# High parts of converted units five steps behind their sums, low parts of weights one step behind, unit stores on GpSimd

## The chip, the cores and the metric

One Trainium2 chip, one of its cores. The core has TensorE (PE; PEld is its weight load), VectorE (DVE), ScalarE (ACT), GpSimd (POOL) and SyncE (SP), which run their own instruction streams in order and wait for one another by semaphores; DMA queues are issued from SP and from POOL. The metric is the device time of one execution in microseconds, as a median of runs. Lower is better.

## The reference

Three stages on 3072 tokens (4 batches of 768) of width 512, all in float32:

```
attention: 8 heads of 64, chunks of 32 queries against 16 + 32 + 8 keys and 8 memory keys, softmax
experts:   tokens with x @ w_skip > 0 go to e = argmax(x @ w_gate);
           x += gate * (relu(x @ w1[e]) @ w2[e])      w1: 512 x 1024, w2: 1024 x 512, 8 experts
dense:     h = max(x @ m1, x @ m2, x @ m3);  out = h @ mo         512 x 768 and 768 x 512
```

The weights of the dense stage (m1, m2, m3, mo) arrive as 64 bit floats.

## The kernel before

To multiply float32 at TensorE's faster rate, each operand is split into a high part (a rounded copy, made by ScalarE) and a low part (operand minus high part, made by VectorE), and a product is three matmuls: high by high, high by low, low by high.

**Experts.** Function `experts` runs eight experts, e = 0 to 7, each with the 256 tokens (two tiles of 128) that were gathered for it. The first product has eight pieces f of 12 matmuls (512 to 1024, into `hp`), the second eight pieces f times two token halves h of 3 matmuls (into `yp`). Between them the tokens of expert e + 1 are transposed (`trans`, tiles `tp`, `xh`, `xl`). The relu leaves `hp` as `hh` (ScalarE) and `hl` (VectorE). `finish(i, y)` multiplies `yp` of the expert before by the gate and adds it to the token rows `xr` on VectorE (L410), and scatters them to `xn` in DRAM from GpSimd (L412); it stands at pieces f = 2 and 3 of the next expert's first product (`FIN`). There is one `yp` per half, so the second product of expert e cannot start before `finish` of expert e - 1 has read it.

**Weights.** Class `Weights` cuts w1 and w2 of an expert into eight units of 128 x 1024. `load` fetches a unit into one of 7 staging tiles (`stga`, `stgb`) from SP, `split` makes the high part (L136, ScalarE) into one of 8 pairs, and `low` the low part (L147, VectorE), after which the staging tile is free again. At each even f the loop calls `K.split(2, upto=i + AHEAD)`, with AHEAD = 5 units, and `K.load()`.

**Conversions.** Beside the experts, class `Convert` turns the 64 bit weights of the dense stage into float32, in units of 128 x 512. The generator `steps` does one unit: an absolute value on ScalarE (`cg<-craw`, L201), six VectorE instructions up to the sum (L203 to L215, tiles `cg` and `cs`), then `lag` steps later the high part (L225, ScalarE) and the low part (L226, VectorE). `feeder` starts a unit every CP = 6.9 steps and advances all units that are under way by one step per call; an expert makes 16 calls (`next(conv)`), 4 in the first product and 12 in the second. Units 0 to 8 stay in SBUF (`unit`); units 9 to 15 go to DRAM (`away`): their high part is made in the one tile `cx`, their low part in `cg` itself, of which there are two, and both are stored (L231). The last expert, e = 7, does its second product half by half, transposes four tiles of tokens for the dense stage meanwhile (`x0`, loaded at L444, transposed at L503), and adds its own result to them by a matmul.

**Dense.** `dense` starts with blocks of 512 tokens j = 0 and 1. `first(j, f)` makes the three products of a piece f of 128 hidden columns, w = 0, 1, 2, each 12 matmuls (L577, into `gp`), and keeps the maximum (`hm`). After each product `step` advances the conversions and the sums that are left. The four token tiles of block 1 are transposed and split by `trans(t)` (`dtp`, `dxh` L566, `dxl` L567) inside `first(0, 1)` and `first(0, 2)`, at the places that `turns` names. `first(1, 0)` needs all four.

The order of the instructions on each engine is the order in which this code calls them.

Of the kernel before, what the change touches and what calls it, by code (L numbers as in the profile page):

```python
# [9 lines left out]
F32 = mybir.dt.float32  # L10
# [19 lines left out]
NEG = -1.0e30  # L30
BIG = float(1 << 20)
TOK0 = 8192.0
AHEAD, C0, CP, LP, LAG = 5, 10, 6.9, 3.2, 2
FIN = (2, 3)
W0, W1, W2, W3, W4 = 7, 0, 4, 4, (0, 3)
CAP = 256
# [118 lines left out]
class Convert:  # L155
# [39 lines left out]
    def steps(self, pool, u, last, lag, fine):  # L195

        nc, V, t = self.nc, self.nc.vector, self.raw.pop(u)
        L, Hw = t[:, :, 0], t[:, :, 1]
        g = pool.tile([128, 512], F32, name="cg", bufs=self.depth)
        gu = g.bitcast(U32)  # L200
        nc.scalar.activation(out=g, in_=Hw.bitcast(F32), func=AF.Abs)  # L201
        yield
        V.tensor_scalar(g, g, 2.0 ** -15, 2.0 ** 16, ALU.max, ALU.mult)  # L203
        V.tensor_scalar(gu, gu, 4, 1, ALU.logical_shift_left, ALU.logical_shift_right)
        if fine:
            yield
        V.scalar_tensor_tensor(out=gu, in0=Hw, scalar=0x80000000, in1=gu, op0=ALU.bitwise_and, op1=ALU.bitwise_or)
        yield
        s = pool.tile([128, 512], U32, name="cs", bufs=self.depth - 1)
        r = s.bitcast(F32)  # L210
        V.tensor_scalar(s, gu, 0xFF800000, None, ALU.bitwise_and)
        V.scalar_tensor_tensor(out=r, in0=L, scalar=2.0 ** -52, in1=r, op0=ALU.mult, op1=ALU.mult)
        if fine:
            yield
        V.tensor_tensor(out=g, in0=g, in1=r, op=ALU.add)  # L215
        if u + self.depth < last:
            self.load(pool, u + self.depth)
        for _ in range(lag):
            yield
        if u < len(self.unit):  # L220
            d = self.unit[u]
            hi, lo = (d[:, c].rearrange("p k f -> p (k f)") if len(d.shape) == 4 else d[:, c] for c in range(2))
        else:
            hi, lo = pool.tile([128, 512], F32R, name="cx", bufs=1), g.bitcast(F32R)
        nc.scalar.copy(hi, g)  # L225
        V.tensor_tensor(out=lo, in0=g, in1=hi.bitcast(F32), op=ALU.subtract)  # L226
        if u < len(self.unit):
            self.done.add(u)
        else:
            for c, x in enumerate((hi, g)):  # L230
                nc.sync.dma_start(out=self.away[u][:, c * 512:(c + 1) * 512], in_=x.bitcast(F32))  # L231

    def feeder(self, pool, units, start, period, lag, fine=True):

# [118 lines left out]
def order(late):  # L353

    if late:
        return [(c, k) for k in range(4) for c in (0, 1)] + [(2, k) for k in range(4)]
    return [(c, k) for k in range(4) for c in range(3)]
# [16 lines left out]
def experts(ac, tc, nc, env):  # L374
    K, C, tab, xn, ident, gidx, sidx = map(env.__getitem__, ("K", "C", "tab", "xn", "ident", "gidx", "sidx"))
# [28 lines left out]
    def passes(ah, al, bh, bl):  # L404
        return ((ah, bh), (ah, bl), (al, bh))
# [3 lines left out]
    def finish(i, y):  # L409
        nc.vector.scalar_tensor_tensor(out=xr[i], in0=y, scalar=tab[:, 1, col(i)], in1=xr[i],  # L410
                                       op0=ALU.mult, op1=ALU.add)
        nc.gpsimd.indirect_dma_start(  # L412
            out=xviews[i], out_offset=bass.IndirectOffsetOnAxis(ap=sidx[:, col(i)], axis=0),
            in_=xr[i], in_offset=None, bounds_check=NT - 1, oob_is_err=False)
# [5 lines left out]
    for e in range(NE):  # L420
        hh = pool.tile([128, 8, 256], F32R, name="hh")
        hl = pool.tile([128, 8, 256], F32R, name="hl")
        for f in range(8):
            if f % 2 == 0:
                i = 8 * e + f // 2
                K.split(2, upto=i + AHEAD)
                K.load()
                wh, wl = (w.rearrange("p (k f) -> p k f", k=4) for w in K.hl[i])
                hp = ps.tile([128, 2, 256], F32, name="hp", bufs=4)
            sl = slice((f % 2) * 128, (f % 2) * 128 + 128)  # L430
            for n, (c, k) in enumerate(order(e == 0 and f == 0)):
                a, b = ((wh, xh[e]), (wl, xh[e]), (wh, xl[e]))[c]
                nc.tensor.matmul(hp[:, f % 2], lhsT=a[:, k, sl], rhs=b[:, k, :], start=(n == 0), stop=(n == 11))  # L433
            if f % 2:
                F = slice(f - 1, f + 1)
                nc.scalar.activation(out=hh[:, F], in_=hp, func=AF.Relu)
                nc.vector.scalar_tensor_tensor(out=hl[:, F], in0=hp, scalar=0.0, in1=hh[:, F].bitcast(F32),  # L437
                                               op0=ALU.max, op1=ALU.subtract)
            if f in FIN and done:
                finish(*done.pop(0))  # L440
            if e == NE - 1 and f == 4:
                x0 = [xrp.tile([128, DM], F32, name="xr") for _ in range(4)]
                for t in range(4):
                    nc.sync.dma_start(out=x0[t], in_=xn[t * 128:(t + 1) * 128, :])  # L444
            if f % 2:
                next(conv, None)
                K.free(i)
        if e + 1 < NE:
            trans(e + 1)
        yp = [ps.tile([128, 512], F32, name=f"yp{h}", bufs=1) for h in range(2)]  # L450

        def gemm2(f, h):
            wh, wl = (w.rearrange("p (f d) -> p f d", f=2) for w in K.hl[8 * e + 4 + f // 2])
            sl = slice(h * 128, h * 128 + 128)
            for n, (a, b) in enumerate(passes(hh[:, f, sl], hl[:, f, sl], wh[:, f % 2, :], wl[:, f % 2, :])):
                nc.tensor.matmul(yp[h], lhsT=a, rhs=b, start=(f == 0 and n == 0), stop=(f == 7 and n == 2))  # L456

        if e == NE - 1:
            break
        for f in range(8):  # L460
            if f % 2 == 0:
                i = 8 * e + 4 + f // 2
                K.split(2, upto=i + AHEAD)
                K.load()
                if f == 2 and 1 <= e and e + 2 < NE:
                    gather(nc, xrp, xr, xn, gidx, e + 2)
            for h in range(2):
                gemm2(f, h)
            next(conv, None)
            if f % 2:  # L470
                next(conv, None)
                K.free(i)
        done = [(2 * e + h, yp[h]) for h in range(2)]
# [56 lines left out]
def dense(ac, tc, nc, env):  # L530
# [6 lines left out]
    C, xn, out, ident, dram = map(env.__getitem__, ("C", "xn", "out", "ident", "dram"))  # L537
# [16 lines left out]
    def load_pair(j, t):  # L554
        load(j, t, [b * 512 + t * 128 for b in (j, j + 1)])
# [120 lines left out]
    steps = [(0, f) for f in range(3)] + [(1, f) for f in range(3)]  # L676
    steps += [(j, f) for f in range(3, 6) for j in range(2)]
    for j, f in steps:
        turns = (2 * f - 2, 2 * f - 1) if j == 0 and f in (1, 2) else ()
        first(j, f, late=(j, f) == (0, 0), step=step, turns=turns)  # L680
        if (j, f) in ((1, 0), (1, 1), (1, 2)):
            load_pair(2, f)
# [797 lines left out]
```

## Time and profile before

| | us |
|---|---|
| median of 3 runs | 766.55 |
| lowest and highest | 765.63 and 767.0 |
| the profiled execution | 766.06 |
| its span, first to last instruction | 764.3 |
| PE busy / DVE busy / ACT busy / POOL busy in it | 707.9 / 546.2 / 292.6 / 133.5 |
| mean granted TensorE clock | 0.983 |

Attention takes the first 167 us, the experts run from there to about 376, the dense stage from there to the end. A row of the timeline shows one instruction: its start, its duration, engine, line, operation, tiles, and in brackets how long its engine had been idle before it and what ended that. Instructions of an engine overlap a little, so what one costs its engine is the distance from its start to the next start, where nothing waits. The profiled execution is 0.49 us below the median.

### The profile page before, as it was taken

The numbers are of one execution on the slowest core, as the hardware profiler recorded it, in microseconds if no ns is written. First come the engines' busy times: TensorE is split into PE (matmuls) and PEld (weight loads), VectorE is DVE, ScalarE is ACT, GpSimd is POOL, SyncE is SP. The second block draws the span as 40 slices with busy tenths as digits, with TensorE's granted clock in tenths as the row PEclk, the third lists the DMA queues.
The fourth block names the chain that finished last, engine by engine and source line by source line (L and its number), as shares of the span: only waits on it lengthen the run. The fifth ranks groups of instructions, "written<-read, shape, count | busy, mean of one in ns | idle before, by whom it ended". The sixth has DMA issues, their size and how long they took to land.

```text
span 764.3 us, 13711 instructions
## 1 busy us (share of the span) xinstructions
PE 707.9 (93%) x5209; PEld 598.6 (78%) x5209; DVE 546.2 (71%) x1027; ACT 292.6 (38%) x498; POOL 133.5 (17%) x273
## 2 busy tenths in 40 slices
PE   6677888969999999989998999999999999999998
PEld 5656677759888899868787888788888888888876
DVE  6455767875799999899689895665666774666641
ACT  5455756534545665344433223450000262000031
POOL 7335546312022121212101111000000000000000
PEclk9999999979999999999999999999999999999999
DMA  8799999838978788873384775212453411333211
GB/s 222 152 243 213 222 229 213 199 124 280 314 253 275 268 267 278 296 252 117 122 330 185 276 257 192 70 56 96 166 194 137 155 67 56 138 138 138 69 42 69
DMA packets 118547, 140.76 MB, mean 184 GB/s; under 512 B 34574, under 2 KB 84750, under 8 KB 118192
## 3 DMA queue, kind: packets, MB, share of 16 engines
q1 hardware_dynamic: 112608, 121.37, 51.7%
q0 software_dynamic: 5872, 18.49, 6.7%
q8 instruction: 42, 0.69, 0.4%
q14 instruction: 25, 0.20, 0.1%
HBM read 103.30 MB, written 32.24 MB: 177 GB/s over the span
## 4 chain that ended last, share of the span: by engine, by line
PE 46%; issue 13%; DMA 11%; DVE 5%; POOL 2%; ACT 1%; SPq 0%; POOLq 0%; DVEq 0%; ACTq 0%
PE gp L761 23%; PE dtp L607 13%; PE gp L577 10%; DMA xr<-xn,gidx 4%; DMA xn<-xr,sidx 3%; DMA craw<-in_moe_w_out_dram 1%; DMA stgb<-in_moe_w_dram 1%; POOL xn L412 1%; DVE wloa L147 1%; PE gp L560 1%; DVE wlob L147 1%; DMA craw<-in_moe_w_dram 1%; DVE hl L437 1%; DMA xs<-xn 1%; DVE xr L410 0%
## 5 line engine op out<-in xcount | busy, mean ns | idle before, releaser
L765 DVE TENSOR_TENSOR tmp<-tmp,gp 128x512 f32<-128x512 f32 x102 | 70.0, 686 | 49.9 <-PE gp L761 49.7
L607 PE MATMUL dtp<-unit,hp 128*128 128x512 f32 x432 | 101.4, 392 | 1.5 <-DVE hp L592 1.5
L607 PEld LDWEIGHTS dtp<-unit,hp 128*128 128x128 f32 x432 | 80.1, 188 | 19.1 <-DVE hp L592 2.3
L433 PE MATMUL hp<-xh,whia 128*128 128x256 f32 x256 | 72.2, 282 | 0.0
L433 PE MATMUL hp<-xh,wloa 128*128 128x256 f32 x256 | 72.0, 281 | 0.0
L433 PE MATMUL hp<-xl,whia 128*128 128x256 f32 x256 | 71.4, 281 | 0.0
L781 ACT COPY tmp<-gp 128x512 f32<-128x512 f32 x18 | 10.6, 588 | 146.4 <-PE gp L761 128.5
L456 PE MATMUL yp<-whib,hh 128*128 128x512 f32 x128 | 52.1, 407 | 5.8 <-DVE xr L410 5.8
L456 PE MATMUL yp<-wlob,hh 128*128 128x512 f32 x128 | 50.7, 396 | 0.0
L456 PE MATMUL yp<-whib,hl 128*128 128x512 f32 x128 | 50.5, 395 | 0.0
L433 PEld LDWEIGHTS hp<-xh,whia 128*128 128x128 f32 x256 | 48.8, 191 | 0.3
L433 PEld LDWEIGHTS hp<-xh,wloa 128*128 128x128 f32 x256 | 48.7, 190 | 0.3
L433 PEld LDWEIGHTS hp<-xl,whia 128*128 128x128 f32 x256 | 48.3, 190 | 0.0
L761 PE MATMUL gp<-unit,set 128*128 128x512 f32 x180 | 46.9, 395 | 0.0
L577 PE MATMUL gp<-x0h,unit 128*128 128x512 f32 x144 | 43.5, 393 | 1.3 <-ACT x0h L522 1.3
L761 PE MATMUL gp<-x0h,unit 128*128 128x512 f32 x144 | 44.5, 390 | 0.0
L577 PE MATMUL gp<-dxh,unit 128*128 128x512 f32 x144 | 44.4, 389 | 0.0
L412 POOL DMA_INDIRECT xn<-xr,sidx x16 | 18.9, 1181 | 132.0 <-DVE xr L410 131.1
L761 PEld LDWEIGHTS gp<-unit,set 128*128 128x128 f32 x180 | 33.7, 187 | 8.2
L1043 PE MATMUL xp<-vs,pb 128*64 128x65 f32 x736 | 28.0, 230 | 10.2 <-DMA vs<-vs 2.7
L592 DVE TENSOR_TENSOR hp<-hm,hp 128x768 fp32r<-128x768 f32 (+2 forms) x26 | 22.9, 895 | 19.8 <-ACT hp L591 19.6
L761 PE MATMUL gp<-unit,unit 128*128 128x512 f32 x144 | 36.5, 389 | 0.0
(272 smaller groups left out, 1619.7 us busy)
## 6 DMA issues: line engine op xcount, KB each, us to landing
stga<-in_moe_w_dram SPq DMA_DIRECT2D x38, 512.0 KB
stgb<-in_moe_w_dram SPq DMA_DIRECT2D x26, 512.0 KB
set<-sum SPq DMA_DIRECT2D x20, 512.0 KB
craw<-in_moe_w_dram SPq DMA_DIRECT2D x18, 512.0 KB
unit<-sum SPq DMA_DIRECT2D x16, 512.0 KB
k<-in_k_dram SPq DMA_DIRECT2D x12, 512.0 KB
q<-in_q_dram SPq DMA_DIRECT2D x12, 512.0 KB
out_dram<-ob SPq DMA_DIRECT2D x24, 256.0 KB
```

What stands on the lines that cost most here:

```text
L147: self.nc.vector.tensor_tensor(out=lo, in0=t, in1=hi.bitcast(F32), op=ALU.subtract)
L412: nc.gpsimd.indirect_dma_start(out=xviews[i], out_offset=bass.IndirectOffsetOnAxis(ap=sidx[:, col(i)], axis=0), in_=xr[i], in_offset=None, ...
L433: nc.tensor.matmul(hp[:, f % 2], lhsT=a[:, k, sl], rhs=b[:, k, :], start=(n == 0), stop=(n == 11))
L437: nc.vector.scalar_tensor_tensor(out=hl[:, F], in0=hp, scalar=0.0, in1=hh[:, F].bitcast(F32), op0=ALU.max, op1=ALU.subtract)
L456: nc.tensor.matmul(yp[h], lhsT=a, rhs=b, start=(f == 0 and n == 0), stop=(f == 7 and n == 2))
L577: nc.tensor.matmul(gp[w], lhsT=l_[:, k, :], rhs=r_[:, k, :], start=(n == 0), stop=(n == 11))
L592: V.tensor_tensor(out=p[:, 1, F], in0=m, in1=p[:, 0, F].bitcast(F32), op=ALU.subtract)
L607: nc.tensor.matmul(op, lhsT=l_, rhs=r_, start=(f == 0 and c == 0), stop=(f == 5 and c == 2))
L761: nc.tensor.matmul(acc, lhsT=l_[:, i, :], rhs=r_[:, i, :], start=(n == 0), stop=(n == 5))
L765: V.tensor_tensor(out=o, in0=x, in1=y, op=ALU.add)
L781: nc.scalar.copy(u, m1)
L1043: nc.tensor.matmul(xps[t][hd // 4][cp * 64:cp * 64 + 64, (hd % 4) * (D + 1):(hd % 4 + 1) * (D + 1)], lhsT=pb[:, hd // 2, cp, hd % 2, :], r ...
```

## The change

The number of steps between the sum of a unit and its high part rises from 2 to 5 in the experts (`LAG`). The stores of the units that go to DRAM are issued from GpSimd, not from SyncE. At each even f, the low parts of the weight units whose high parts were made at the even f before are made first, then new high parts (`split` with `low=False`), then the loads. In the dense stage, tile 2 of block 1 is transposed after w = 2 of `first(0, 1)` and tile 3 after w = 0 of `first(0, 2)`; before, they stood after w = 0 and w = 1 of `first(0, 2)`.

```diff
-AHEAD, C0, CP, LP, LAG = 5, 10, 6.9, 3.2, 2
+AHEAD, C0, CP, LP, LAG = 5, 10, 6.9, 3.2, 5
...
             for c, x in enumerate((hi, g)):
-                nc.sync.dma_start(out=self.away[u][:, c * 512:(c + 1) * 512], in_=x.bitcast(F32))
+                nc.gpsimd.dma_start(out=self.away[u][:, c * 512:(c + 1) * 512], in_=x.bitcast(F32))
...
                 i = 8 * e + f // 2
-                K.split(2, upto=i + AHEAD)
+                K.low()
+                K.split(2, upto=i + AHEAD, low=False)
                 K.load()
...
                 i = 8 * e + 4 + f // 2
-                K.split(2, upto=i + AHEAD)
+                K.low()
+                K.split(2, upto=i + AHEAD, low=False)
                 K.load()
...
-        turns = (2 * f - 2, 2 * f - 1) if j == 0 and f in (1, 2) else ()
+        turns = {1: (0, 1, 2), 2: (3,)}.get(f, ()) if j == 0 else ()
```

On VectorE, around `finish` of expert 0 (tiles `xr`), early in the first product of expert 1, this stands in a row before (`wlob` are low parts of weights, `unit<-cg` the low part of conversion unit 0):

```order
L147 TENSOR_TENSOR wlob_3189<-stgb_3183,whib_3188 128x1024
L437 SCALAR_TENSOR_TENSOR hl<-hp,hh 128x512
L226 TENSOR_TENSOR unit_3166<-cg,unit_3166 128x512
L147 TENSOR_TENSOR wlob_3191<-stgb_3184,whib_3190 128x1024
L410 SCALAR_TENSOR_TENSOR xr<-yp_3388,tab,xr 128x512
L437 SCALAR_TENSOR_TENSOR hl<-hp,hh 128x512
L410 SCALAR_TENSOR_TENSOR xr<-yp_3389,tab,xr 128x512
```

and this in the changed kernel (its lines below L426 are one or two higher):

```order
L147 TENSOR_TENSOR wlob_3187<-stga_80,whib_3186 128x1024
L438 SCALAR_TENSOR_TENSOR hl<-hp,hh 128x512
L147 TENSOR_TENSOR wlob_3189<-stgb_3183,whib_3188 128x1024
L410 SCALAR_TENSOR_TENSOR xr<-yp_3386,tab,xr 128x512
L438 SCALAR_TENSOR_TENSOR hl<-hp,hh 128x512
L410 SCALAR_TENSOR_TENSOR xr<-yp_3387,tab,xr 128x512
```

The low part of unit 0 has moved behind the two `xr`, and each low part of weights stands where its forerunner stood.

On GpSimd, in experts 5 to 7, seven pairs of stores now stand among the gathers (L368) and the scatters (L412); this is the stretch from the scatters of expert 4 to those of expert 6, of the changed kernel:

```order
L412 DMA xn<-xr,sidx 3072x512 [waits DVE_49]
L231 DMA away_3159<-cx 128x512 [waits Activation_49]
L231 DMA away_3159<-cg 128x512 [waits DVE_49]
L368 DMA xr<-xn,gidx 128x512 [waits DMASW1_49,DMASW0_49,PE_49]
L368 DMA xr<-xn,gidx 128x512 [waits PE_49]
L231 DMA away_3160<-cx 128x512 [waits Activation_49]
L231 DMA away_3160<-cg 128x512 [waits DVE_49]
L231 DMA away_3161<-cx 128x512 [waits Activation_49]
L231 DMA away_3161<-cg 128x512 [waits DVE_49]
L412 DMA xn<-xr,sidx 3072x512 [waits DMASW4_49,DMASW5_49,DMASW2_49,DVE_49]
```

Before, the four gathers and scatters of this stretch followed one another with nothing between.

On VectorE, at the end of `first(0, 2)`, before:

```order
L639 TENSOR_TENSOR sl<-sr,sh 128x1024
L226 TENSOR_TENSOR unit_5244<-cg,unit_5244 128x512
L624 TENSOR_TENSOR ga<-unit_3168 128x512
L624 TENSOR_TENSOR gb<-unit_3169 128x512
L567 TENSOR_TENSOR dxl<-dtp,dxh 128x4x128
L581 TENSOR_TENSOR hm_5253<-hm_5253,gp_5450 128x512
L203 TENSOR_SCALAR cg<-cg 128x512
L204 TENSOR_SCALAR cg<-cg 128x512
...
L634 TENSOR_TENSOR sr<-ga,sr 128x256
L567 TENSOR_TENSOR dxl<-dtp,dxh 128x4x128
```

and in the changed kernel:

```order
L641 TENSOR_TENSOR sl<-sr,sh 128x1024
L569 TENSOR_TENSOR dxl<-dtp,dxh 128x4x128
L226 TENSOR_TENSOR unit_5244<-cg,unit_5244 128x512
L626 TENSOR_TENSOR ga<-unit_3168 128x512
L626 TENSOR_TENSOR gb<-unit_3169 128x512
L569 TENSOR_TENSOR dxl<-dtp,dxh 128x4x128
L583 TENSOR_TENSOR hm_5253<-hm_5253,gp_5457 128x512
```

The last `dxl` has moved ahead of eight instructions, to the place of the one before it.

## Rows read from the trace of the kernel before

**Rows 1.** PE's waits, whole span: who waited for whom, total us, times, longest

```profile
PE yp L456 <- DVE xr L410: 5.8, 8, 3.5
PE gp L577 <- DVE dxl L567: 2.5, 1, 2.5
...
PE tp L503 <- DMA xr<-xn: 1.1, 1, 1.1
```

**Rows 2.** PE's timeline at those waits: start us, us, instruction, idle before

```profile
210.36 0.47 PE L456 MATMUL yp<-whib,hh 128*128 128x512 f32 x1 [0.77 <-DVE xr L410]
...
282.13 0.48 PE L456 MATMUL yp<-whib,hh 128*128 128x512 f32 x1
...
332.59 0.61 PE L456 MATMUL yp<-whib,hh 128*128 128x512 f32 x1 [3.48 <-DVE xr L410]
...
336.35 0.39 PE L456 MATMUL yp<-whib,hh 128*128 128x512 f32 x1
336.58 0.39 PE L456 MATMUL yp<-wlob,hh 128*128 128x512 f32 x1
...
406.14 0.50 PE L577 MATMUL gp<-dxl,unit 128*128 128x512 f32 x1 [2.47 <-DVE dxl L567]
```

**Rows 3.** Busy time, granted clock and DMA share of two microseconds after the longest wait

```profile
334.00:336.00 2.00, 2.00 (x6) 1.58 (x6) 2.00 (x4) 2.00 (x3) 1.64 (x1) 0.50 1.00 360
```

**Rows 4.** DVE's timeline in the experts: first conversion, finishes, longest wait

```profile
201.53 0.43 DVE L203 TENSOR_SCALAR cg<-cg 128x512 f32<-128x512 f32 x1 [4.93 <-ACT cg L201]
...
207.72 0.68 DVE L226 TENSOR_TENSOR unit<-cg,unit 128x512 fp32r<-128x512 f32 x1
208.33 1.23 DVE L147 TENSOR_TENSOR wlob<-stgb,whib 128x1024 fp32r<-128x1024 f32 x1
209.47 0.75 DVE L410 SCALAR_TENSOR_TENSOR xr<-yp,tab,xr 128x512 f32<-128x512 f32 x1
...
322.76 0.69 DVE L226 TENSOR_TENSOR cg<-cg,cx 128x512 fp32r<-128x512 f32 x1 [1.86 <-ACT cx L225]
...
331.70 0.74 DVE L410 SCALAR_TENSOR_TENSOR xr<-yp,tab,xr 128x512 f32<-128x512 f32 x1
...
355.30 0.74 DVE L410 SCALAR_TENSOR_TENSOR xr<-yp,tab,xr 128x512 f32<-128x512 f32 x1
```

**Rows 5.** DVE's waits from 205 to 356 us: total us, times, longest

```profile
DVE cg L226 <- ACT cx L225: 2.6, 2, 1.9
DVE wlob L147 <- ACT whib L136: 1.9, 3, 0.9
DVE unit L226 <- ACT unit L225: 1.4, 2, 0.7
DVE wloa L147 <- ACT whia L136: 0.8, 3, 0.3
```

**Rows 6.** ACT's timeline: three instructions that waited for a DMA

```profile
200.83 0.67 ACT L201 ACTIVATE cg<-craw 128x512 f32<-128x512 f32 x1 [6.69 <-DMA craw<-in_moe_w_dram]
...
322.11 0.62 ACT L225 CAST cx<-cg 128x512 fp32r<-128x512 f32 x1 [6.73 <-DMA away<-cx]
...
400.02 0.68 ACT L201 ACTIVATE cg<-craw 128x512 f32<-128x512 f32 x1 [1.49 <-DMA craw<-in_moe_w_out_dram]
```

**Rows 7.** SP's queue: the store that ScalarE waited for at 322.11

```profile
315.02 0.46 SPq L231 DMA_DIRECT2D away<-cx  x1
```

**Rows 8.** DVE's timeline in the dense stage: the low parts of tiles 2, 3

```profile
401.21 0.69 DVE L567 TENSOR_TENSOR dxl<-dtp,dxh 128x512 fp32r<-128x512 f32 x1 [0.40 <-ACT dxh L566]
...
405.40 0.68 DVE L567 TENSOR_TENSOR dxl<-dtp,dxh 128x512 fp32r<-128x512 f32 x1
```

**Rows 9.** Tile `sum`: stores from POOL in the dense stage (ns min/median/max), landing

```profile
L640 POOL DMA_DIRECT2D sum<-sh  x9: 547/550/619, 396.3 to 467.7; - x9
...
DMA to landing us min/median/max: 2.9/3.4/8.0
```

**Rows 10.** Line 412: scatters from POOL (ns min/median/max)

```profile
L412 POOL DMA_INDIRECT xn<-xr,sidx x16: 982/1034/1684, 210.5 to 381.2; - x16
```

## The prediction, made before the changed kernel was run

> **What bounds the kernel now.** I read the waits first: after attention TensorE hardly stops, and the list of its waits is short [rows 1]. Its second products wait eight times, 5.8 us in all, for `xr`, that is for `finish` on VectorE to release `yp`; it waits once, 2.5 us, for the last `dxl` of block 1, and once, 1.1 us, for the tokens `x0` from DRAM. Everything else in experts and dense is matmul after matmul, so only these waits, and what they cost in clock, can be won.
>
> Then I read TensorE's timeline at the waits [rows 2]. The first expert that waits does so for 0.77 us at 210.36; the long one is 3.48 us, before 332.59, in expert 6; the dense one is 2.47 us before 406.14. The long wait costs more than itself. In the two microseconds 334 to 336 the granted clock is 0.50, the lower of the two levels, 1.2 GHz [rows 3]. From 332.59 to 336.35 nine matmuls start, 3.76 us; at the distance that follows, 0.23 us (336.35 to 336.58), they would take 2.07. So 1.7 us are lost to the clock.
>
> Then VectorE, since it is the one waited for [rows 4]. It starts its first conversion only at 201.53, having idled 4.93 us for ScalarE, which had waited 6.69 us for the load of `craw` [rows 6], and it finishes expert 0 at 209.47, too late for 209.59, where TensorE arrives. From this first `xr` to the seventh (355.30) are 145.8 us. In them VectorE waits 6.7 us [rows 5], so its work is 139.1, or 23.2 per expert. TensorE needs 47.0 us for two experts (282.13 to 329.11, where the wait of 3.48 begins), 23.5 each [rows 2]. The two engines are matched to a per cent: VectorE never recovers its late start, and each of its waits comes out on TensorE. The largest is the one of 1.86 us at 322.76, for `cx` [rows 4]. ScalarE could make that high part only at 322.11, 6.73 us idle, because `cx` is one tile and its last store, issued at 315.02 from SP, had not landed [rows 6, 7].
>
> **Part 1, high parts five steps late.** This removes the waits of VectorE for a unit's high part: ScalarE was waiting for the sum just made, VectorE then for ScalarE, 2.6 + 1.4 us [rows 5]; and because ScalarE no longer stands in that queue, the high parts of weights behind it come earlier. It also moves the low part of unit 0 behind the first two `xr`. Its cost is 0.61 us (207.72 to 208.33), so the first `xr` comes 0.6 us earlier [rows 4], and 0.77 becomes about 0.2.
>
> **Part 2, low parts of weights one step late.** The other waits of VectorE, 1.9 + 0.8 us, are for high parts of weights made just before [rows 5]. A step of lead is about a 2.9 us (23.5 us for 8 units), more than the longest of them, 0.9, so I cost them at nothing. No instruction is added. What it costs is a staging tile for a step: each load is issued 2.9 us later. From a low part to the high part of the unit that takes its tile are then 6 steps, 17.5 us, less the 7 or so by which VectorE may run behind, say 10; the longest landing in the rows is 8.0 [rows 9]. So the loads stay covered. In the start, where loads wait for one another, fewer of them now stand ahead of the first `craw`: that load can come earlier by up to the time of one load. At the 360 GB/s of a full DMA [rows 3] two such loads of 512 KB take 2.9 us; I bound the gain of VectorE's first conversion by 0 and 2 us and need none of it.
>
> With the waits gone, VectorE (23.2) gains a little on TensorE (23.5) in each expert, from a start that is level. So all eight waits shrink to some tenths at most: minus 5.8, of which I leave 0.2, and minus 1.7 of clock. What is late next is VectorE again, with some tenths to 1 us in hand.
>
> **Part 3, stores on GpSimd.** Fourteen stores leave SP, where weight loads stood behind them, and enter POOL's queue. Queued behind them there are the gather for expert 7 and the scatters of experts 5 and 6. A direct store takes 0.55 us of POOL [rows 9], two per unit 1.1; POOL has little else to do there, and the gather's tokens are not needed for most of an expert. The new wait is another: with five steps of lag, `cg` of a unit is freed later, its store must land before ScalarE may start the unit after next, and high parts of weights queue behind that on ScalarE, low parts on VectorE. In most units 10 us of VectorE's work lie between. In two places, where both fall into one second product (units 10 to 12 in expert 5, 12 to 14 in expert 6), there are only three or four conversion instructions at about 0.6 and two low parts at 1.14 (208.33 to 209.47) [rows 4]: 4.1 and 4.7 us. Against that stand 0.55 to issue, 3.4 to land [rows 9] and 0.67 for the absolute value [rows 6], 4.6 in all: VectorE waits 0.5 and 0. With the longest landing, 8.0, it waits 5.1 and 4.5. I take plus 0.4, by the median row, which is of stores of twice the size from the same engine.
>
> On such stores the rows show 0.547 to 0.619 us on POOL, though VectorE ran its conversions beside them [rows 9]. The Trainium skill speaks against this part: its page "SBUF — State Buffer", section "SBUF: two separate sides", warns that GpSimd cannot write descriptors while VectorE is in a two-port mode, and in "A bandwidth-pool intuition that's wrong" gives 3.1 us where 0.62 is the time alone. By that figure, an estimate, a pair of stores would hold POOL 6.2 us, and the sum would be worse by some 10 us; the rows do not bear it out.
>
> **Part 4, turns.** The last `dxl` takes the place of the one before it. That one started at 401.21, this one at 405.40 [rows 8]; TensorE reached the need at 403.67 (406.14 less 2.47) [rows 2]. At 401.21 plus 0.69 it is ready with 1.7 us to spare, so all 2.47 go. Its `dxh` still stands on ScalarE behind the absolute value that waited for its load until 400.02 [rows 6]; if that load is later by more than 1.7 us against TensorE, the wait comes back. The removed wait is not given back later by VectorE: the `gp` tiles are double.
>
> **Part 5, the tokens `x0`.** They are loaded after the scatters of expert 6's result. If VectorE is only as early against TensorE as before, the 1.1 us stay; if it is 2 us earlier by the earlier `craw`, they go. Nearest is neither; I take minus 0.6 between 0 and 1.1.
>
> **Sum.** -5.8 + 0.2 - 1.7 - 2.5 + 0.4 - 0.6 = -10.0. The profiled execution took 766.06, so 756.1; it was 0.49 below the median, so **756.6 us**. Bounds of the terms alone: 755.4 (all of `x0`, no new wait, no remainder) to 758.5.
>
> **Rivals.** First, VectorE stays the bound: 23.2 against 23.5 leaves no room, the small waits of the experts 1 to 4, 2.4 us (5.8 less 3.48), stay, and so does `x0`. For it speaks that VectorE's idle time is all it has; against it that TensorE's own arrival sets the pace once it no longer waits. Or the dense wait comes back by a late load. Each gives about 759.
>
> Second, stores land slowly. The store of 315.02 needed until 322.11, 6.6 us from the end of its issue, on a full DMA [rows 6, 7]. Then VectorE loses 3.7 and 3.1 us at the two places; with 1 us in hand TensorE waits 2.7 and, after the clock's share (half of a wait, as 1.7 of 3.48), loses 4.0, and some 2.5 more in expert 7: 763.
>
> Third, slower than before: POOL's queue. If a store takes as long there as the longest scatter, 1.7 us [rows 10], and lands in 8.0, the two places cost 1.7 + 1.7 + 8.0 + 0.67 less 4.1 and 4.7, that is 8.0 and 7.4; TensorE waits 7.0 and about 5.7 and loses half as much again in clock, 19 us, against 10 won: 775. It decides from about 9.5 us between low part and free tile, where the losses reach the gain. Against it are the 27 stores from POOL in the dense stage, whose group of nine stays below 0.62 [rows 9]. This is also where the skill's rule would lead.
>
> Fourth, no change: waits form again at every `xr` in the same size, because the load of `craw` comes later than before; 766.
>
> **How the numbers follow.** Forecast (755.3 to 758.0) 0.48; all of `x0` and a longer lead, 755, 0.09; first rival, 758 to 760, 0.18; second, 760 to 764.5, 0.15; fourth 0.04; third 0.06. The range leaves out the third, the fourth, the upper part of the second and a little below: 754.8 to 762.5. About 0.2%, 1.5 us, is what a measurement of this kernel can tell from no change; faster by more than that is 0.90 by these cases; I keep 0.88, 0.05 the same, 0.07 slower.
>
> **What would show it.** Right: no wait of TensorE for `xr` above 0.5 us, the granted clock at 1.00 through expert 6, no wait for `dxl`, VectorE without waits for `cx`, `unit`, `whib`, `whia`; the first `xr` at about 209 or before. Wrong: ScalarE waiting for `away<-cg` or `away<-cx`, with VectorE idle for `cg` at L203 behind it; TensorE waiting for low parts of weights in expert 0; ScalarE waiting for weight loads; stores of more than 1 us on POOL. Most of all the forecast fails if VectorE, at 99% of TensorE's pace, finds any new wait.

## The result, and the profile after

The changed kernel takes 758.25 us, the median of 4 runs (756.63 to 759.13), beside 766.09 for the kernel before; the quotient of the two medians is 0.9898. The ratio on record, which is estimated in another way, is 0.9866, 95% interval 0.9828 to 0.9904, and the interval takes in both. The forecast was 756.6, with a range of 754.8 to 762.5. The profiled execution took 759.13 us (span 757.4), 0.88 above its median; that of before took 766.06. The two profiles are 6.9 us apart.

TensorE's waits, whole span, in the form of [rows 1] (who waited for whom, total us, times, longest):

```profile
PE yp L457 <- ACT xh L398: 2.2, 1, 2.2
...
PE yp L457 <- DVE xr L410: 0.5, 2, 0.2
```

The waits for `dxl` and for `x0` are gone, and so are those for `xr` in the experts 1 to 4 but for one of 0.23. One long wait is left, where the longest was before, in expert 6. TensorE's timeline there, and the granted clock behind it, in the forms of [rows 2, 3]:

```profile
329.33 0.47 PE L457 MATMUL yp<-whib,hh 128*128 128x512 f32 x1 [2.23 <-ACT xh L398]
...
330.50 0.50 PE L457 MATMUL yp<-whib,hh 128*128 128x512 f32 x1 [0.23 <-DVE xr L410]
330.83 0.59 PE L457 MATMUL yp<-wlob,hh 128*128 128x512 f32 x1
...
334.20 0.43 PE L457 MATMUL yp<-whib,hh 128*128 128x512 f32 x1
334.47 0.40 PE L457 MATMUL yp<-wlob,hh 128*128 128x512 f32 x1
```

```profile
332.00:334.00 2.00, 2.00 (x6) 1.54 (x5) 2.00 (x4) 1.16 (x2) 1.04 (x2) 0.50 0.68 208
```

The clock falls to 0.50 again: nine matmuls take 3.64 us (330.83 to 334.47), at a distance of 0.23 they would take 2.07, so 1.6 us are lost beside the wait of 2.2. The name in the bracket misleads. The copy `xh` that it names, 328.71 plus 0.60, ended only at 329.31, when TensorE had already begun to load this matmul's weights:

```profile
329.30 0.19 PEld L457 LDWEIGHTS yp<-whib,hh 128*128 128x128 f32 x1 [2.44 <-ACT xh L398]
```

What ended just before is `xr`, at 328.44 plus 0.74, and VectorE's timeline [as rows 4] tells why it is late:

```profile
314.74 0.69 DVE L226 TENSOR_TENSOR cg<-cg,cx 128x512 fp32r<-128x512 f32 x1
...
318.26 1.22 DVE L147 TENSOR_TENSOR wloa<-stga,whia 128x1024 fp32r<-128x1024 f32 x1
321.11 0.43 DVE L203 TENSOR_SCALAR cg<-cg 128x512 f32<-128x512 f32 x1 [1.63 <-ACT cg L201]
...
322.57 0.69 DVE L226 TENSOR_TENSOR cg<-cg,cx 128x512 fp32r<-128x512 f32 x1 [0.57 <-ACT cx L225]
...
328.44 0.75 DVE L410 SCALAR_TENSOR_TENSOR xr<-yp,tab,xr 128x512 f32<-128x512 f32 x1
```

VectorE idles 1.63 and 0.57 us here, 2.2 in all, for ScalarE. POOL's and ScalarE's timelines between the two:

```profile
315.72 0.56 POOL L231 DMA_DIRECT2D away<-cg  x1 [3.35 <-DVE cg L226]
```

```profile
320.41 0.68 ACT L201 ACTIVATE cg<-craw 128x512 f32<-128x512 f32 x1 [7.97 <-DMA away<-cg]
...
321.92 0.62 ACT L225 CAST cx<-cg 128x512 fp32r<-128x512 f32 x1
```

The low part of unit 10 ends at 315.43, its store is issued from 315.72 to 316.28, and only at 320.41 may ScalarE begin unit 12 in the same tile `cg`. The view of the chain that ended last shows the store from the start of its issue to its landing (start, us):

```profile
315.72 4.62 DMA away<-cg
```

This is the first of the two tight places that part 3 of the prediction names; the second, in expert 6, made no wait. VectorE has one more wait on the way to expert 6. It stands in expert 5's first product, for `hh`, behind an absolute value for which ScalarE had waited until 296.93, for the load of `craw`:

```profile
299.08 0.69 DVE L438 SCALAR_TENSOR_TENSOR hl<-hp,hh 128x512 fp32r<-128x512 f32 x1 [0.75 <-ACT hh L437]
```

```profile
296.93 0.68 ACT L201 ACTIVATE cg<-craw 128x512 f32<-128x512 f32 x1 [5.47 <-DMA craw<-in_moe_w_dram]
```

How the 14 stores fare (tile `away`: ns min/median/max; landing in us, counted from the start of the issue, which the trace gives for nine of them):

```profile
L231 POOL DMA_DIRECT2D away<-cx x7: 539/585/618, 305.1 to 361.1; - x7
L231 POOL DMA_DIRECT2D away<-cg x7: 539/557/576, 305.7 to 361.8; - x7
...
DMA to landing us min/median/max: 2.5/2.9/4.9
```

**A measure that the start doesn't disturb.** Ahead of the experts all kernels here run the same code, yet in their 14 profiles expert 0's first `yp` matmul starts anywhere from 183.9 to 189.9 us. Why is not worked out here; the mean granted clock ahead of it does not order them (0.91 in the earliest profile, 0.93 in the latest). So I compare three stretches: VectorE's, from the first finish (`xr`) to the seventh, as the prediction did; TensorE's, from the first `yp` matmul to the first `gp` matmul; and from there to the end of the span. In the changed kernel the first is 140.5 (before 145.8 [rows 4]):

```profile
209.54 0.74 DVE L410 SCALAR_TENSOR_TENSOR xr<-yp,tab,xr 128x512 f32<-128x512 f32 x1
...
350.05 0.75 DVE L410 SCALAR_TENSOR_TENSOR xr<-yp,tab,xr 128x512 f32<-128x512 f32 x1
```

All kernels, by these stretches of their profiled executions (us), and their times against the kernel before on the same chip:

| kernel | xr to xr | yp to gp | gp to end | median | ratio to before, 95% |
|---|---|---|---|---|---|
| before | 145.8 | 189.8 | 388.2 | 766.09 | |
| changed | 140.5 | 184.4 | 385.4 | 758.25 | 0.9866 (0.9828 to 0.9904) |
| changed, again | 140.9 | 185.6 | 385.2 | 758.95 | 0.9861 (0.9827 to 0.9895) |
| part 1 undone (lag 2) | 140.8 | 185.4 | 385.3 | 758.27 | 0.9877 (0.9844 to 0.9910) |
| part 2 undone | 143.3 | 187.8 | 385.4 | 760.35 | 0.9899 (0.9863 to 0.9935) |
| part 3 undone (stores on SP) | 142.0 | 191.0 | 385.5 | 763.54 | 0.9929 (0.9904 to 0.9954) |
| part 4 undone (turns) | 140.5 | 184.7 | 389.8 | 762.45 | 0.9925 (0.9901 to 0.9949) |
| part 2 alone | 142.6 | 186.9 | 388.6 | 765.78 | 0.9973 (0.9950 to 0.9997) |
| part 3 alone | 143.8 | 189.0 | 391.1 | 766.38 | 0.9963 (0.9940 to 0.9987) |
| lag 3 | 138.6 | 183.0 | 385.3 | 756.12 | 0.9855 (0.9823 to 0.9887) |
| lag 4 | 142.6 | 187.4 | 385.4 | 761.69 | 0.9915 (0.9886 to 0.9943) |
| lag 7 | 148.4 | 192.4 | 385.3 | 766.11 | 0.9977 (0.9957 to 0.9998) |
| three `cg` | 137.3 | 181.0 | 385.5 | 756.46 | 0.9846 (0.9818 to 0.9874) |
| three `cg`, later `x0` | 137.2 | 179.0 | 385.6 | 754.08 | 0.9815 (0.9786 to 0.9843) |

The medians of before that belong to the experiments were 767.8 to 768.6, so different rows are compared by their ratios. As in the first row, a ratio is not exactly the quotient of the medians beside it; the two differ by up to 0.3%, in each row by less than the interval reaches to either side.

### The profile page after: what moved, and what is told of

Same layout as the page of the kernel before. It is cut to its first block, busy times and chain, and to the rows that moved or that the text cites. A ratio compares the mean times of both kernels' runs of the same rounds, so it can differ in the third digit from the quotient of the medians.

```text
span 757.4 us, 13676 instructions
## 1 busy us (share of the span) xinstructions
PE 711.2 (94%) x5209; PEld 603.2 (80%) x5209; DVE 543.9 (72%) x1027; ACT 292.7 (39%) x498; POOL 142.8 (19%) x287
## 4 chain that ended last, share of the span: by engine, by line
PE 55%; DVE 14%; DMA 3%; issue 3%; ACT 1%; SPq 0%; DVEq 0%; ACTq 0%
PE gp L763 23%; PE gp L579 13%; PE dtp L609 13%; PE yp L457 3%; DVE wlob L147 3%; DVE wloa L147 3%; DVE hl L438 2%; DMA craw<-in_moe_w_dram 2%; PE hp L434 1%; DMA stgb<-in_moe_w_dram 1%; DVE xr L410 1%; DVE cg L207 1%; PE gp L562 1%; DVE xl L399 1%; DVE cs L212 1%
## 5 line engine op out<-in xcount | busy, mean ns | idle before, releaser
L412 POOL DMA_INDIRECT xn<-xr,sidx x16 | 19.0, 1189 | 102.9 <-DVE xr L410 101.0
L594 DVE TENSOR_TENSOR hp<-hm,hp 128x768 fp32r<-128x768 f32 (+2 forms) x26 | 22.9, 895 | 19.8 <-ACT hp L593 19.6
L980 POOL TENSOR_SCALAR kw<-kt 128x448 f32<-128x448 f32 (+1 forms) x96 | 33.5, 377 | 8.0 <-PE sc L1000 4.8
```

Source lines behind the costliest of these rows:

```text
L412: nc.gpsimd.indirect_dma_start(out=xviews[i], out_offset=bass.IndirectOffsetOnAxis(ap=sidx[:, col(i)], axis=0), in_=xr[i], in_offset=None, ...
L594: V.tensor_tensor(out=p[:, 1, F], in0=m, in1=p[:, 0, F].bitcast(F32), op=ALU.subtract)
L980: e.tensor_scalar(o, i_, 1.0, 1.0, ALU.mult, ALU.mult)
```

## The experiments

My theory after the result: what is left in expert 6 is ScalarE's wait for the store of `cg`, with two tiles and a lag of five steps. The rivals: VectorE's own work is the bound (the prediction's first rival), or another part of the change carries the gain.

**The changed kernel again.**

> The changed kernel itself again, beside the three others on one chip. Theory: as in its first profile 198 us from the first hp matmul to the first gp matmul and 385.3 from there to the end of the span, with a wait of TensorE of 2 to 3.5 us for xr in expert 6 that follows a wait of ScalarE for the store of cg; 8 us faster than the kernel before. Rival (the wait in expert 6 was an accident of one execution): no wait above 0.7 us there, and some 3.5 us less.

```profile
329.37 0.47 PE L457 MATMUL yp<-whib,hh 128*128 128x512 f32 x1 [2.63 <-ACT xh L398]
```

```profile
332.00:334.00 2.00, 2.00 (x10) 1.66 (x9) 2.00 (x4) 1.21 (x2) 1.08 (x2) 1.00 0.68 201
```

The wait is no accident: 2.63 us at the same place. But the clock stayed at 1.00 this time. The 1.6 us so kept were not won: TensorE came earlier to the tokens `x0` and waited 1.2 us at their transposes, where it had not waited in the first profile. Both spans are 757.4.

**Three tiles `cg`.** The same order of work, one more tile; the room comes from two tables that are given back early.

```diff
...
-        g = pool.tile([128, 512], F32, name="cg", bufs=self.depth)
+        g = pool.tile([128, 512], F32, name="cg", bufs=self.depth + fine)
```

> The changed kernel with three tiles cg instead of two in the experts (room for it comes from two small tables that are given back after their last use); the order of all work stays. Theory (ScalarE waits for the store of cg to land): its wait for the tile goes, VectorE's wait of 2.2 us in expert 5 goes, TensorE's waits in expert 6 (2.2 and 0.2) and its half clock (1.5) go: 3 to 4 us faster than the changed kernel, 754.3 to 755.3. Rival one (VectorE's work is the bound): within 0.5 us of the changed kernel. Rival two (the single tile cx is next late, since its store lands as late as that of cg): VectorE waits 1 us or more for cx instead, 756 to 758.

TensorE's waits of the experts' stretch, all of those ahead of the dense stage; VectorE's first and seventh finish; TensorE's first `yp` matmul of experts 5 and 6:

```profile
PE tp L507 <- DMA xr<-xn: 1.1, 2, 0.8
```

```profile
209.83 0.75 DVE L412 SCALAR_TENSOR_TENSOR xr<-yp,tab,xr 128x512 f32<-128x512 f32 x1
...
347.11 0.74 DVE L412 SCALAR_TENSOR_TENSOR xr<-yp,tab,xr 128x512 f32<-128x512 f32 x1
```

```profile
304.22 0.47 PE L459 MATMUL yp<-whib,hh 128*128 128x512 f32 x1
...
327.29 0.47 PE L459 MATMUL yp<-whib,hh 128*128 128x512 f32 x1
```

No wait for `xr` is left anywhere, VectorE waits for nothing between 205 and 356 us, and its stretch is 137.3, or 22.9 per expert; TensorE goes at 23.07 per expert (304.22 to 327.29). From the first `yp` to `gp` it takes 3.4 us less than the changed kernel in its first profile and 4.6 less than in its second; by the ratios the whole time is 1.2 to 1.5 us shorter, less than the intervals can tell apart. The theory holds for the waits: the 2.2 us are gone. Gone with them is the 0.75 for `hh`: ScalarE's absolute value there ran at 294.67, not at 296.93, as the load of `craw` was there sooner, and why it was is not shown. So not all of the gain is the wait for `cg`. The second rival (`cx` next late) doesn't show in this profile. Another 1.1 went to the wait for `x0`, which is back.

**Other lags.** The number 5 becomes 3, 4 or 7.

```diff
-AHEAD, C0, CP, LP, LAG = 5, 10, 6.9, 3.2, 5
+AHEAD, C0, CP, LP, LAG = 5, 10, 6.9, 3.2, 7
```

> The changed kernel with high parts seven steps behind their sums. Theory (cg's store): two steps less between the store of a unit and the next use of its tile, some 2 us; VectorE's wait for cg in expert 5 grows from 2.2 to above 4, a second one of about 2 comes in expert 6, and TensorE waits for xr there with half a wait more in clock: 3 to 6 us slower than the changed kernel, 761 to 764. Rival (VectorE's work alone is the bound): within 0.7 us of the changed kernel.

VectorE's two waits, and TensorE's:

```profile
314.25 0.43 DVE L203 TENSOR_SCALAR cg<-cg 128x512 f32<-128x512 f32 x1 [4.34 <-ACT cg L201]
...
326.23 0.43 DVE L203 TENSOR_SCALAR cg<-cg 128x512 f32<-128x512 f32 x1 [4.56 <-ACT cg L201]
```

```profile
333.92 0.77 PE L457 MATMUL yp<-whib,hh 128*128 128x512 f32 x1 [7.30 <-DVE xr L410]
```

For ScalarE's idle time ahead of them (8.65 and 8.89 us, before the absolute values at 313.56 and 325.52) the timeline names no releaser; the stores of `cg` issued at 307.28 and 320.83, of the units that had the tiles before, landed at 313.49 and 325.45. Two steps more in the lag, and VectorE waits 8.9 us instead of 2.2, at this place and one more, and a third time, 1.77 us at 348.77, in expert 6; nearly all the gain is gone (0.9977). As expected, and larger.

> The changed kernel with high parts three steps behind their sums. Theory (cg's store): the wait of VectorE for cg in expert 5 goes wholly; against that ScalarE may again stand waiting for sums of VectorE, by some tenths each: 754.5 to 756.5. Rival (VectorE's own work is the bound, the less lag the more waits): slower than the changed kernel by 0.5 to 2 us, 759 to 760.

The wait for `cg` is gone, VectorE's stretch is 138.6, and 0.7 us of small waits for `xr` remain: as the theory said. The stretch is 1.3 longer than with three tiles and the long lag.

> The changed kernel with high parts four steps behind their sums instead of five. Theory (what is left in expert 6 is the landing of a store of cg that stands one step too close): a step is about 1 us in a second product, so VectorE's wait for cg in expert 5 falls from 2.2 to about 1 us, TensorE's wait in expert 6 from 2.2 to about 1, with less clock lost: 1.5 to 2.5 us faster than the changed kernel, 755.7 to 756.8. Rival (VectorE's own work, 23.2 us against 23.5 per expert, makes the wait in expert 6): within 0.5 us of the changed kernel.

This came out wrong. TensorE waits 3.45 us in expert 6, more than with five steps. VectorE's, POOL's and ScalarE's timelines:

```profile
325.65 0.69 DVE L226 TENSOR_TENSOR cg<-cg,cx 128x512 fp32r<-128x512 f32 x1 [4.08 <-ACT cx L225]
```

```profile
317.05 0.56 POOL L231 DMA_DIRECT2D away<-cg  x1 [1.32 <-DVE cg L226]
```

```profile
323.49 0.67 ACT L201 ACTIVATE cg<-craw 128x512 f32<-128x512 f32 x1 [9.95 <-DMA away<-cg]
```

ScalarE waited for the same tile. Expert 5's second product starts at 306.63 here and at 303.85 in the changed kernel, so against TensorE the store was issued 1.45 us earlier (10.42 behind it, not 11.87). But from the end of its issue to ScalarE's start it took 5.9 us (317.61 to 323.49) instead of 4.1. So a step less is worth nothing if the landing moves by more than a step. Here the store followed 1.9 us behind the gather for expert 7, in the changed kernel 4.7; that this made it slow is argued, not shown.

**Each part undone, or alone.**

```diff
...
-                K.low()
-                K.split(2, upto=i + AHEAD, low=False)
+                K.split(2, upto=i + AHEAD)
... (the same at the second place)
```

> The changed kernel with part 2 undone: low parts of weights right behind their high parts again. Theory (each part takes away its own waits of VectorE): 1.9 + 0.8 us of waits for whib and whia come back on VectorE, and VectorE has less than 1 us in hand, so 1.5 to 3.5 us slower than the changed kernel with the clock, 760 to 761.7. Rival (with the high parts five steps late ScalarE is early enough, and the waits for whib and whia don't come back): within 0.5 us of the changed kernel.

```profile
321.99 1.22 DVE L147 TENSOR_TENSOR wlob<-stga,whib 128x1024 fp32r<-128x1024 f32 x1 [3.73 <-ACT whib L136]
```

```profile
330.68 0.76 PE L456 MATMUL yp<-whib,hh 128*128 128x512 f32 x1 [4.53 <-ACT whia L136]
```

2.4 to 2.8 us are lost on VectorE's stretch, as expected, though not where expected: the small waits of before don't return one by one. At the tight place a high part of a weight stands behind the waiting absolute value on ScalarE, and its low part now follows at once on VectorE, which waits 3.73 us instead of 2.2. In the same way it waits 2.17 at 297.85, behind the late `craw`, where the changed kernel waits 0.75.

> The kernel before with part 2 alone: low parts of weights one step behind their high parts; high parts of conversions two steps behind, stores on SP. Theory (each part takes its own waits away, and VectorE's waits come out on TensorE): the 2.7 us of waits of VectorE for whib and whia go, those for cx and unit stay, TensorE's waits for xr fall from 5.8 to 2.5 to 4.5: 2 to 3.5 us faster than the kernel before. Rival (part 2 is what carries the gain in the experts): the waits for xr fall below 1.5 us, 5 us or more faster than before.

VectorE's stretch falls by 3.3 us and TensorE's waits for `xr` to 3.0 in all, the longest 2.1: the theory, 2.9 us off the stretch from `yp` to `gp`.

> The changed kernel with part 1 undone: high parts two steps behind their sums, the other parts as changed. Theory (the lag took the waits for unit, cx and the early low part away): the first xr comes 0.6 us later, VectorE waits some 3 us for unit and cx again over the seven experts, TensorE waits for xr in several experts and in expert 6: 2 to 5 us slower than the changed kernel, 760 to 763. Rival (the low parts moved a step, part 2, carry the gain, and the lag only brings the wait for the tile cg in expert 5): the wait of 2.2 us in expert 6 goes with its clock, 1.5, and little comes in its place: 754.5 to 757.

Neither. The time is that of the changed kernel (0.9877, beside 0.9866 and 0.9861), and VectorE's stretch is that of the changed kernel within the difference of its two profiles (140.8 beside 140.5 and 140.9). The small waits come back (0.9 us for `xr`, 1.0 for `hh`, 1.2 for `wlob`), and the wait for `cg` goes. With two tiles `cg`, part 1 as a whole brings nothing that these runs can tell. A lag of two with three tiles was not run.

```diff
-                nc.gpsimd.dma_start(out=self.away[u][:, c * 512:(c + 1) * 512], in_=x.bitcast(F32))
+                nc.sync.dma_start(out=self.away[u][:, c * 512:(c + 1) * 512], in_=x.bitcast(F32))
```

> The changed kernel with part 3 undone: the stores of converted units are issued by SP again, all else as changed. Theory (the wait of ScalarE for the tile cg in expert 5 is the landing of a store, whichever queue issues it; weight loads queue behind the stores on SP): the wait in expert 5 stays within 1.5 us of its 2.2, SP's loads are covered, so 757 to 760. Rival (GpSimd's stores land later than SP's): the wait of VectorE for cg falls below 1 us and TensorE's wait in expert 6 with it, 755 to 756.5. Rival the other way (loads of weights wait behind stores that wait for VectorE): TensorE or ScalarE waits for weight loads, 761 or more.

The theory held for its own place: VectorE waits 2.92 us for `cg` in expert 5, beside 1.63. The time is the rival's the other way, by a road that I had not seen. SP's queue, then ScalarE and TensorE:

```profile
357.11 1.75 SPq L445 DMA_DIRECT2D xr<-xn  x4
358.96 0.37 SPq L231 DMA_DIRECT2D away<-cx  x1
```

```profile
364.43 0.62 ACT L225 CAST cx<-cg 128x512 fp32r<-128x512 f32 x1 [8.51 <-DMA away<-cx]
```

```profile
365.65 0.81 PE L505 MATMUL tp<-ident,xr 128*128 128x128 f32 x4 [3.11 <-ACT stgb L507]
```

The four loads of `x0` wait on SP for expert 6's scatters; the store of a `cx` that was made at 355.31 stands behind them until 358.96. The next `cx` waits for it until 364.43, behind that the copies of the tokens, and TensorE 3.11 us for those.

> The kernel before with part 3 alone: stores of converted units from GpSimd. Theory (a store lands as slowly from either queue; the one tile cx makes the wait of 1.9 us): within 1 us of the kernel before. Rival (SP's queue, with weight loads and the loads of x0 between the stores, was what made cx late): VectorE's wait for cx falls below 0.7 us and TensorE's wait in expert 6 from 3.5 to below 2: 2 to 4 us faster than before.

The rival: VectorE's longest wait for `cx` falls from 1.86 to 0.73 and TensorE's in expert 6 from 3.48 to 1.11; its longest for `xr` is now 1.50, in expert 1:

```profile
208.62 0.47 PE L456 MATMUL yp<-whib,hh 128*128 128x512 f32 x1 [1.50 <-DVE xr L410]
...
328.78 0.47 PE L456 MATMUL yp<-whib,hh 128*128 128x512 f32 x1 [1.11 <-DVE xr L410]
```

In the kernel before, ScalarE made the `cx` ahead of that wait here:

```profile
312.28 0.62 ACT L225 CAST cx<-cg 128x512 fp32r<-128x512 f32 x1 [4.73 <-DVE cg L215]
```

With the stores on POOL, ScalarE's rows of that `cx` and the next, and POOL's row of its store:

```profile
310.85 0.62 ACT L225 CAST cx<-cg 128x512 fp32r<-128x512 f32 x1 [4.83 <-issue]
...
318.34 0.62 ACT L225 CAST cx<-cg 128x512 fp32r<-128x512 f32 x1 [4.41 <-DVE cs L212]
```

```profile
311.76 0.58 POOL L231 DMA_DIRECT2D away<-cx  x1 [5.24 <-ACT cx L225]
```

Before, `cx` was done at 312.90 and its store issued at 315.02 [rows 7], 2.1 us later, since SP is a queue and a load of weights stood ahead of it, issued at 314.56; on POOL it goes 0.3 us after the end. VectorE's stretch shrinks by 2.1. In the whole time that is a part only (0.9963): the dense wait for `dxl` was 3.7 in this profile.

```diff
...
-        turns = {1: (0, 1, 2), 2: (3,)}.get(f, ()) if j == 0 else ()
+        turns = (2 * f - 2, 2 * f - 1) if j == 0 and f in (1, 2) else ()
```

> The changed kernel with part 4 undone: the last turn of the tokens of block 1 stands again where it stood before. Theory (the turn alone took the dense wait away): the wait of 2.5 us for the last dxl comes back, so 8 less 2.5 = 5.3 us faster than the kernel before, about 760.7. Rival (the dense wait went because ScalarE and VectorE reach the dense stage earlier now): the wait stays below 0.5 us, about 758.4, 7.7 us faster than before.

```profile
401.21 0.80 PE L579 MATMUL gp<-dxl,unit 128*128 128x512 f32 x1 [2.67 <-DVE dxl L569]
```

```profile
402.00:404.00 2.00, 2.00 (x7) 1.52 (x6) 1.93 (x4) 0.00 (x0) 0.52 (x1) 0.50 0.47 186
```

The theory: the wait is back, and here with half clock behind it, so the stretch from `gp` to the end is 4.4 us longer.

**A version that beats both.** Three `cg`, and the tokens' transposes two steps later, since their wait was left:

```diff
-XT, YT = 7, 3
+XT, YT = 9, 3
... (and the third tile, as above)
```

> The changed kernel with three tiles cg, and the transposes of the tokens x0 two steps of the last second product later (1.4 us). Theory: no wait for cg and no wait for xr in the experts, and the wait of 1.1 us for the tokens x0, which the three tiles alone left, goes: 193 to 194 us from the first hp matmul to the first gp matmul, 4 to 5 us faster than the changed kernel. Rival (the copies of the tokens on ScalarE and the sums behind the last product are then late): the wait moves to gp for x0h, and the time stays that of the three tiles, 3 to 3.5 faster than the changed kernel.

From the first `hp` matmul to the first `gp` matmul (171.9 to 364.9) 193.0 us, as the theory said. No wait for `xr`, `cg` or `x0` is left, and the five full experts from 208.99 to 324.38 take 23.06 to 23.12 us each. On the same chip: 754.08 us (752.27 to 755.57), the changed kernel 758.95 (754.49 to 760.0).

## Why the prediction was right, and where it was not

The forecast was 1.65 us below the median and its range held. The mechanism held in part, and that the time held is partly luck. Of the signs of being right that the prediction names, some came: TensorE does not wait for `dxl`, and VectorE does not wait for `unit`, `whib` or `whia`. Others failed: TensorE waits 2.2 us for `xr`, VectorE 0.57 for `cx`, and in the first profile the clock falls in expert 6. The first sign of being wrong came to the letter: ScalarE waiting for `away<-cg`, with VectorE idle at L203 behind it. Another came in small: in the second profile TensorE waits 0.27 us for `wlob` in expert 0. What this lost was in part made up by terms that brought more than counted; and 758.25 lies just above the band of the forecast's own case (755.3 to 758.0), in that of the first rival, whose mechanism did not come: the waits of the experts 1 to 4 are gone. Term by term:

- **Part 4, -2.5.** Right: -2.8 from `gp` to the end. The last `dxl` is made at 397.24 and first used 2.2 us later.
- **The waits for `xr` in the experts 0 to 4.** From the first `yp` matmul of expert 0 to that of expert 5 the gain is 3.1 us (119.3 to 116.2), where the prediction counted 2.3 (5.8 less 3.48; it says 2.4) less 0.2. The wait list names no gap under some tenths, and those went too. Behind this is a figure that was off: TensorE's 23.5 us per expert, read from [rows 2], held such gaps; it needs 23.07. VectorE, 23.2 by the working, needs 22.9 (137.3 for six with three `cg`; 140.5 less 2.95 of waits in the changed kernel). The two differ by 0.2 instead of 0.3, so the verdict on the two engines (matched to a per cent) stands.
- **The new wait, +0.4. This is the step that failed.** The place was named, the cover of 4.1 us was right (VectorE works from 315.34 to 319.48), and that ScalarE's queue and then VectorE's would stand behind it, too. Too small was the price. The landing of 3.4, the median of [rows 9], was 4.6 here, counted alike, that is from the start of the issue (315.72 to 320.33). Since the count begins there, the 0.55 to issue stood in the sum twice, which by chance covered part of the 1.2 that were missing; from the end of the issue to ScalarE's start it was 4.1 (316.28 to 320.41). What counts at a tight place is the landing there, with the DMA at a share of 1.05 beside it, not a median. Left out were 0.3 from the end of the low part to the issue, and a high part of a weight and `cx` behind the absolute value on ScalarE, for which VectorE waited another 0.57. So 2.2 instead of 0.5. And the lead of some tenths to 1 us that should have taken some of it was none: TensorE waited the same 2.2. VectorE had lost 0.75 of it just before, by the wait for `hh` at 299.08, a load that came late and that no term held.
- **The clock, -1.7.** It hangs on the step above. In one profile 1.6 were lost again, in the other none.
- **`x0`, -0.6.** The 1.1 went in the first profile, where the lower clock made TensorE 1.6 later; in the second, at the full clock, 1.2 of wait came back, half of it for the tokens, half for ScalarE's copies of them. So the sum counted twice what is one: `x0` hangs on expert 6's finish on VectorE, so time that TensorE saves ahead of it is not won until VectorE is earlier. This is the first rival (VectorE stays the bound) in small; it is the reason for the last experiment.
- **Part 3, costed at no gain.** Wrong in favour of the change. The 6.6 us in [rows 6, 7] are a slow landing (the DMA was at a share of 0.81 there, not full, as the prediction says); the 2.1 us that the store had stood in SP's queue before were not looked at. And with part 1 the stores stand later, beside the loads of `x0`; on SP this would have cost 6 us or so (191.0 beside 184.4 and 185.6).
- **Part 1, costed at a gain.** Its waits did go (2.6 + 1.4 on VectorE, with the 0.57 for `cx` of the new wait in their place), and the first finish came 0.6 us earlier against the first conversion (202.21 to 209.54, before 7.94 [rows 4]), to the tenth. But undoing it changes nothing that the runs can tell, since it brings the wait for `cg`. Part 2, costed with 2.7 us, is worth 2.4 to 3.3 on VectorE's stretch.
- **`craw`.** The prediction bounded an earlier first load by 0 and 2 us and needed none: against the start of expert 0's second product, ScalarE's first absolute value did not clearly move (13.9 and 14.6 us behind it in the two profiles, before 14.5).

Profile against profile: forecast -10.0. Expert 6 gave 1.0 (50.8 to 49.8 from expert 5's first `yp` to expert 7's) where 4.8 were counted (3.48 + 1.7 - 0.4); the experts ahead 1.0 more than counted, the end of the experts 0.7 more (19.7 to 18.4, with 0.6 counted), the dense stage 0.3 more; expert 0's second product began 1.3 us later. That is -10.0 + 3.8 - 1.0 - 0.7 - 0.3 + 1.3 = -6.9, and 6.9 was measured. Of the 1.3, 1.1 lie ahead of the first `hp` matmul, in the stretch that all kernels share. Two more things the working left out or took too small. [rows 1] skips TensorE's wait of 1.3 us for `x0h` at the start of the dense stage, which is there before and after alike. And what a measurement can tell, 0.2%, was too little: the interval came out at 0.4% to either side.

The second rival's price, 763, supposed 6.6 us of landing, counted from the end of the issue, at both places; the longest of the nine known was 4.9, with the issue. The third, POOL's queue, did not come: the stores took 0.54 to 0.62 us on POOL with VectorE busy beside them. This is where the Trainium skill ("SBUF — State Buffer", "A bandwidth-pool intuition that's wrong") would have led with its 3.1 us. The trace shows nothing of that size, and the longest of these stores on POOL in any profile is 0.80; but the page's figure is of a DMA beside a `tensor_copy` of VectorE, which it counts among the two-port operations, and whether VectorE's instructions beside these stores ran in such a mode no run shows. On the landing, its page "DMA: Bandwidth & Descriptors", section "Anatomy of one DMA — SWDGE (gpsimd) path", gives a fit of 2.0 us plus bytes over 436e3; for 256 KB that is, as an estimate, 2.6 us. The shortest landing here, 2.5, agrees; the one that mattered was 4.6.

## What to carry to other kernels

Before moving work behind a store, write down for each reuse of the tile: end of the producer, start of the issue, landing at that load of the DMA (the longest in the rows, not the median), and everything that stands behind the waiting instruction on its engine; one more tile at that place was worth more than the whole lag. A store that waits on a queue with loads is late before it is issued: look at when its source was ready. And when two engines are matched, a wait that vanishes at one place may only have moved to where the other engine is next needed, so follow the chain to its end before adding it to the sum.

## What the runs showed of the hardware

- **A wait of TensorE costs half clock at times, and not by its length alone.** Behind a wait of 2.23 us the granted clock fell to 0.50 (first profile), behind 2.63 us at the same place of the same kernel it stayed at 1.00; behind 2.67 us for `dxl` it fell to 0.50, behind 2.47 in the kernel before it did not. Of all waits between 2 and 3 us in the experts and at the dense stage's start, over the 14 profiles, those of 2.06, 2.21, 2.23, 2.67 and 2.87 us were followed by a fall, those of 2.47, 2.63 and 2.82 were not. The price, where it fell in expert 6 of the changed kernel, was 1.6 us. The Trainium skill ("TensorE: Matmul & The Clock Gate", Part 1, "What's actually happening") says of a kernel's start that the number of matmuls at the lower clock differs from run to run; these profiles show that behind a pause in the middle, too, one run of a kernel can differ from the next, of which it is not said there.
- **The landing of equal stores of 256 KB from one queue** went from 2.5 to 4.9 us in one profile and from 2.3 to 8.5 in another (lag 3), counted from the start of the issue. It goes with what else the DMA engines do. In the eleven profiles with these stores on POOL the trace gives 82 landings: where the DMA share in the 2.5 us from the start of the issue was below 0.5, the median was 2.5 us (14 stores, 2.3 to 4.0); where it was 0.95 or more, 4.9 (24 stores, none below 4.0). No run varied the share alone.
